# One load per float64 weight piece in 1 KB packets, the power of two in two ScalarE passes, and the sums of pair 4 off TensorE

## The chip, the cores and the metric

The kernel runs on one core of one Trainium2 chip. The metric is the device time of one execution in microseconds (us). The engines, by the names that the profile uses: PE is TensorE (matmuls; PEld is its weight load), DVE is VectorE, ACT is ScalarE, POOL is GpSimd and SP is SyncE, which here only issues DMAs. A name with a q (SPq, POOLq) is an engine's queue of DMA issues. Every engine works through its own instructions strictly in the order in which they were written; engines wait for each other by semaphores.

## The reference

Two blocks in a row. The first is attention with a threshold: for 8 batches of 8 heads, 576 positions and 64 values a head,

```
scores = scale * q @ k.T
thresh = max(scores, axis=-1) - tau
scores = where(scores >= thresh, scores, -1e9)
attn   = exp(scores - max(scores));  attn /= sum(attn) + 1e-9
x      = attn @ v                     # then (B,H,S,D) -> (4608, 512)
```

The second is a feed-forward block on the 4608 rows of x:

```
h = x @ w_in                          # 512 -> 2048
g = h * 1 / (1 + exp(-1.702 * h))
out = g @ w_out                       # 2048 -> 512
```

q, k and v are float32. The two weight matrices reach the kernel as float64, and the kernel turns them into float32 itself, from their bits.

## The kernel before

**Attention.** Work goes by pairs of heads: four pairs a batch, 32 in all. The first four pairs (batch 0) go a straight way, in 20 units (pair n, tile t of 128 queries): scores on PE (L668), row maxima (L678) and a bias (L683) on DVE, the mask (L689) and the exponentials with their sums (L697) on ACT, a transposition on PE (L708, L709), copies of it on ACT (L718, L726), a small reciprocal on DVE (L732, L733), its spread over partitions by matmuls with the identity (`straight_den`, L745) and the values (`straight_values`, L758) on PE. `straight_spread` (L764, ACT) copies the spread reciprocals into the block's input xT and `straight_place` (L768, DVE) multiplies the values into it. Both matmul groups of a unit write the same PSUM tile, `small`, of which there are two buffers, shared with the feed-forward block.

From pair 4 on the scores stay transposed. PE makes them (L540), ACT copies them out (`keep`, L557), DVE takes maxima by groups of 32 (L563) and folds them, and for nearly all pairs the row of maxima goes to DRAM (L613) and comes back broadcast over 64 partitions (`row_in`, L622; the profile writes arena<-row). DVE subtracts it (`sub`, L627), ACT masks (L633) and exponentiates (L637), PE multiplies with the values (L779). The sums of the exponentials take one of two ways. Pairs from 5 on: DVE adds by groups (L563 again), `turn_sums` (L828 to L833) makes the reciprocals, `sums_out` (L838) writes them to DRAM and `sums_in` (L845) reads them back broadcast, both on SP. Pair 4 alone: `sums_by_pe`, 36 matmuls with a matrix of ones (tile den, L779), then `one_row` (L802, L806) and `spread_sums` (L854, L856) on DVE. `place_x` (L871) multiplies values by reciprocals into xT. From pair 7 on PE's values of pair n-2 alternate with the scores of pair n.

**Feed-forward.** 18 blocks of 256 rows. Blocks 0 and 1 are plain: `mm1_0` (L929) for 16 chunks of 128 hidden values, tanh on ACT (L895), gelu on DVE (L935), then `mm2` (L908). Chunks 4c to 4c+3 of the hidden values need four pieces of w_in; the second layer needs w_out by rows. Block 2 and later blocks (L886, gelu L898, L1080) use Strassen-like products whose weight sums are made by ACT (L1036) and by accumulating DMAs from POOL (L1040, 1 MB each). Block 2 holds rows of batch 1, so it needs pairs 4 to 7 placed.

**Weights.** There are 32 pieces of 128 x 512 float64 values, 16 of w_in and 16 of w_out. A piece is loaded twice from POOL's queue (`load_w`, L466 and L467): once as words and once shifted by three bytes, so that the top 28 bits of the fraction line up in a word. The pieces lie in six places until they are converted: four in rows of w_out that are not yet filled ("stage"), two in the arena ("w64"). DVE takes the exponent (`cv_ex`, L477), ACT makes the power of two from it with one Relu (`cv_power`, L485, on every other word), DVE cuts and signs the fraction (`cv_frac`, L491 and L495) and multiplies (`cv_end`, L503). The first six loads wait until k of pair 3 has been prepared (`hold`).

**Order.** Nothing is ordered by hand. `run_in_order` is a planner: it plays the tasks through with given costs, takes on each engine the ready task of lowest rank, and writes the instructions in that order. Ranks are a base for each pair or piece (S_RANK, W_RANK) plus an offset for each kind of task (EARLY, SECOND, LATER, CV). The tasks of the feed-forward block on PE have the last rank (LAST) and so fill what attention leaves. Transfers are modelled by two movers, SP's (DMS) and the weights' (DMW), that share bandwidth by SHARE.

Of the kernel before, what the change touches and what calls it, by code (L numbers as in the profile page):

```python
# [10 lines left out]
FP32 = mybir.dt.float32  # L11
# [8 lines left out]
P = 128  # L20
# [10 lines left out]
def kernel(  # L31
# [98 lines left out]
    for x in ("P0", "P1", "P2", "PT0", "PT1"):  # L130
# [3 lines left out]
        "load_qk": 3.49,  # L134
        "load_v": 61.83,
        "prep": 15.43,
        "straight_bias": -0.96,
        "straight_copy": -11.35,
        "straight_copy1": 16.32,
        "straight_den": 8.82,  # L140
        "straight_exps": 28.06,
        "straight_mask": -43.64,
        "straight_max": 14.96,
        "straight_place": -2.45,
        "straight_rc": 26.0,
        "straight_scores": -15.67,
        "straight_spread": 28.02,
        "straight_turn": 5.62,
        "straight_values": 34.4,
        "w_sum": 16.49,  # L150
    }
    SECOND = {
        "exps": 53.1,
        "in_groups": 125.36,
        "keep": 24.5,
        "load_qk": 15.38,
        "load_v": 40.57,
        "mask": 51.96,
        "one_row": 31.95,
        "over_halves": -45.57,  # L160
        "over_tiles": 26.99,
        "place_x": 1.35,
        "prep": 9.24,
        "row_in": 57.1,
        "row_out": -10.1,
        "scores_run": -13.37,
        "spread_sums": 38.44,
        "sub": 49.29,
        "sums_by_pe": 66.1,
        "sums_in": 49.6,  # L170
        "sums_out": -47.62,
        "turn_rows": -10.91,
        "turn_sums": 11.87,
        "values": 17.4,
    }
    LATER = {
        "exps": 41.63,
        "in_groups": 59.97,
        "keep": 8.55,
        "load_qk": 30.71,  # L180
        "load_v": 52.56,
        "mask": 61.02,
        "over_halves": -20.34,
        "over_tiles": 9.26,
        "place_x": -2.55,
        "prep": -8.58,
        "row_in": -50.04,
        "row_out": -53.37,
        "scores_run": 26.7,
        "sub": 15.31,  # L190
        "sums_in": 13.02,
        "sums_out": 33.45,
        "turn_rows": 7.35,
        "turn_sums": 21.37,
        "values": 50.74,
        "x_sum": 55.75,
    }
# [10 lines left out]
    MODES = {"scores_run": 1, "values": 1, "sums_by_pe": 1, "straight_scores": 1, "straight_values": 2, "straight_den": 2}  # L208
# [15 lines left out]
    SHARE = (0.055, 0.3)  # L224
# [98 lines left out]
    rebias = const.tile([P, 1], FP32, name="rebias")  # L323
    JOINT = 7
# [101 lines left out]
    cv, turn = {}, {"w64": 0}  # L426
# [3 lines left out]
    PER_STAGE = NFC // STAGES  # L430

    def stage(i):
# [6 lines left out]
    for x in range(STAGES):  # L439
        limits[f"stage{x}"] = 1  # L440

    def load_w(i):
        dst, src, c, j = pieces[i]
        dram = src[ts(c, P), ts(j, WC)]
        if not wide:
            nc.gpsimd.dma_start(out=dst[:, c, ts(j, WC)], in_=dram)
            return


        x = stage(i)  # L450
        if x is None:
            o = 4 * WC * (turn["w64"] % 2)
            turn["w64"] += 1
            t, t3 = (
                arena[:, ds(o + 2 * WC * y, 2 * WC)].bitcast(U32).rearrange(
                    "p (c w) -> p c w", w=2
                )
                for y in range(2)
            )
        else:  # L460
            rows = [w_out[:, ds(PER_STAGE * x + 2 * y, 2), :] for y in range(2)]
            t, t3 = (
                r.rearrange("p a b -> p (a b)").bitcast(U32).rearrange("p (c w) -> p c w", w=2)
                for r in rows
            )
        nc.gpsimd.dma_start(out=t.rearrange("p c w -> p (c w)"), in_=dram.bitcast(U32))  # L466
        nc.gpsimd.dma_start(  # L467
            out=t3.rearrange("p c w -> p (c w)").bitcast(U8)[:, 0 : 8 * WC - 3],
            in_=dram.bitcast(U8)[:, 3 : 8 * WC],
        )  # L470
        cv[i] = t[:, :, 1], t[:, :, 0], t3[:, :, 0]
# [3 lines left out]
    def cv_ex(i):  # L475
        hi, ex, _ = cv[i]
        nc.vector.tensor_scalar(  # L477
            out=ex, in0=hi, scalar1=20, scalar2=0x7FF,
            op0=ALU.logical_shift_right, op1=ALU.bitwise_and,
        )  # L480

    def cv_power(i):

        ex = cv[i][1].bitcast(I32)
        nc.scalar.activation(out=ex, in_=ex, func=AF.Relu, scale=2.0**23, bias=rebias)  # L485

    def cv_frac(i):


        hi, _, frac = cv[i]  # L490
        nc.vector.tensor_scalar(  # L491
            out=frac.bitcast(I32), in0=frac.bitcast(I32), scalar1=0x0FFFFFFF,
# [659 lines left out]

    SUMS_BY_PE = (4,)
    BY_DMA = (0, 1, *range(3, NP))
    SUMS_BY_DMA = range(5, NP)
    LEAD = 6
# [457 lines left out]
```

## Time and profile before

| | |
|---|---|
| median of 3 runs | 1329.69 us (1327.19 to 1330.22) |
| the profiled execution | 1330.04 us, span 1328.3 us |
| mean granted TensorE clock | 0.988 |
| PE busy | 1282.8 us (97%) |
| DVE, ACT, POOL busy | 981.8 us (74%), 662.1 us (50%), 250.3 us (19%) |
| DMA | 102.91 MB; POOL's software queue 37.74 MB, SP's queue 63.40 MB |

Times in the profile are us from the first instruction. A row of a group of instructions reads: line, engine, operation, out<-in with shapes, count | busy us, mean ns of one | idle time of that engine just before them, and what ended it. A busy PE is not a PE at its peak, since matmuls overlap and their ends are modelled. Idle time of an engine that does not set the end costs nothing.

### The profile page before, as it was taken

How to read it: one execution, taken by the hardware profiler on the slowest of the kernel's cores; microseconds unless marked ns; L12 is line 12 of the kernel's file. 1: busy time of each engine (PE TensorE's matmuls, PEld its weight loads, DVE VectorE, ACT ScalarE, POOL GpSimd, SP SyncE). 2: the span in 40 equal slices, each digit the busy share in tenths (PEclk: the TensorE clock that was granted, in tenths of full speed). 3: DMA queues.
4: the chain of work that ended last, by engine and by line, in shares of the span. 5: the costliest groups of instructions: out<-in, count | busy, mean ns of one | idle time of the engine just before them, and what ended most of it. 6: DMA issues, size and time to landing. Idle time of an engine off the chain costs nothing.

```text
span 1328.3 us, 23115 instructions
## 1 busy us (share of the span) xinstructions
PE 1282.8 (97%) x9212; PEld 999.9 (75%) x9212; DVE 981.8 (74%) x1640; ACT 662.1 (50%) x922; POOL 250.3 (19%) x296
## 2 busy tenths in 40 slices
PE   6798989897999999999999999999999999999998
PEld 3576664456777777777888777777777878888887
DVE  6888887987788888777787777778887873652642
ACT  6897665676455555555455545455555540210210
POOL 2111210002113120212120202112111217120120
PEclk9899999898999999999999999999999999999999
DMA  8786767256221222222222222212222110000000
GB/s 173 211 303 172 259 185 126 62 108 107 59 67 49 68 48 66 48 54 53 71 55 71 55 70 55 65 42 57 59 46 57 33 53 9 17 0 25 9 0 32
DMA packets 194949, 102.91 MB, mean 77 GB/s; under 512 B 160282, under 2 KB 173338, under 8 KB 194842
## 3 DMA queue, kind: packets, MB, share of 16 engines
q1 hardware_dynamic: 181114, 63.40, 20.4%
q0 software_dynamic: 11360, 37.74, 9.5%
q8 instruction: 72, 1.18, 0.4%
q10 hardware_dynamic: 2368, 0.30, 0.2%
q14 instruction: 35, 0.29, 0.1%
HBM read 87.51 MB, written 9.69 MB: 73 GB/s over the span
## 4 chain that ended last, share of the span: by engine, by line
PE 78%; DVE 7%; DMA 7%; SPq 4%; ACT 3%; issue 1%; DVEq 0%; ACTq 0%
PE ops L1080 24%; PE hps L886 22%; PE pv L779 8%; PE ps L540 8%; PE ps L994 4%; PE ps L1080 4%; PE ops L994 3%; PE hps L929 3%; SPq L393 2%; DMA arena<-row 2%; DVE arena L627 2%; DVE part L563 2%; DMA arena<-in_k_dram 2%; DMA row<-flat 1%; PE rest L758 1%
## 5 line engine op out<-in xcount | busy, mean ns | idle before, releaser
L563 DVE TRANSPOSE_TENSOR_REDUCE part<-arena 128x36 f32<-128x1152 f32 x275 | 334.5, 1238 | 46.3 <-ACT arena L557 36.9
L886 PE MATMUL hps<-xT,w_in 128*128 128x256 f32 x1536 | 339.7, 382 | 6.9 <-DVE arena L898 6.9
L886 PEld LDWEIGHTS hps<-xT,w_in 128*128 128x128 f32 x1536 | 292.3, 191 | 53.2 <-DVE arena L898 7.9
L633 ACT ACTIVATE arena<-arena 128x1152 f32<-128x1152 f32 (+1 forms) x140 | 147.6, 1059 | 155.6 <-DVE arena L627 155.5
L1080 PE MATMUL ops<-w_out,arena 128*128 128x256 f32 x896 | 202.7, 381 | 1.0 <-DVE arena L898 0.9
L627 DVE TENSOR_TENSOR arena<-arena 128x1152 f32<-128x1152 f32 (+1 forms) x140 | 178.1, 1313 | 26.7 <-DMA arena<-row 26.6
L557 ACT COPY arena<-ps 128x576 f32<-128x576 f32 x252 | 149.9, 642 | 94.6 <-PE ps L540 92.8
L1080 PEld LDWEIGHTS ops<-w_out,arena 128*128 128x128 f32 x896 | 169.1, 190 | 28.7 <-DVE arena L898 3.1
L637 ACT ACTIVATE arena<-arena,shift,scl 128x1152 f32<-128x1152 f32 (+1 forms) x140 | 174.5, 1250 | 3.0
L1046 POOL TENSOR_TENSOR arena<-arena 128x256 f32<-128x256 f32 x56 | 50.3, 897 | 644.7 <-DVE arena L898 542.9
L540 PE MATMUL ps<-arena 64*64 64x288 f32 x2016 | 150.5, 411 | 5.2 <-ACT arena L557 5.2
L895 ACT ACTIVATE th<-hps 128x512 f32<-128x512 f32 x112 | 66.3, 592 | 170.9 <-PE hps L886 156.6
L1080 PE MATMUL ops<-arena 128*128 128x256 f32 x672 | 150.6, 380 | 0.0
L779 PE MATMUL pv<-arena 64*64 64x288 f32 x2016 | 147.7, 407 | 0.0
L1080 PEld LDWEIGHTS ops<-arena 128*128 128x128 f32 x672 | 127.2, 190 | 19.3 <-issue 2.2
L540 PEld LDWEIGHTS ps<-arena 64*64 64x64 f32 x2016 | 74.2, 135 | 57.1 <-ACT arena L557 15.9
L1102 DVE SCALAR_TENSOR_TENSOR osb<-ops,osb 128x256 f32<-128x256 f32 x98 | 39.3, 413 | 100.0 <-PE ops L1080 93.8
L779 PEld LDWEIGHTS pv<-arena 64*64 64x64 f32 x2016 | 74.7, 134 | 50.9 <-issue 10.0
L898 DVE SCALAR_TENSOR_TENSOR arena<-th,hps 128x512 f32<-128x512 f32 x96 | 64.4, 671 | 38.6 <-ACT th L895 38.4
L929 PE MATMUL hps<-xT,w_in 128*128 128x256 f32 x256 | 62.9, 400 | 7.7 <-DVE arena L935 7.4
L929 PEld LDWEIGHTS hps<-xT,w_in 128*128 128x128 f32 x256 | 49.4, 199 | 19.3 <-DVE arena L935 8.9
L524 DVE STREAM_TRANSPOSE arena<-arena 128x576 f32<-128x576 f32 x60 | 42.9, 746 | 22.1 <-DMA arena<-in_k_dram 11.1
(134 smaller groups left out, 1267.2 us busy)
## 6 DMA issues: line engine op xcount, KB each, us to landing
arena<-in_v_dram SPq DMA_DIRECT2D x112, 144.0 KB
arena<-in_q_dram SPq DMA_DIRECT2D x128, 72.0 KB
out_dram<-osb SPq DMA_DIRECT2D x36, 256.0 KB
arena<-in_k_dram SPq DMA_DIRECT2D x124, 72.0 KB
arena<-row SPq DMA_DIRECT2D x56, 144.0 KB
arena<-row_s SPq DMA_DIRECT2D x54, 144.0 KB
w_out<-in_moe_w_in_dram POOLq DMA_DIRECT2D x12, 512.0 KB, 8.9
arena<-in_moe_w_out_dram POOLq DMA_DIRECT2D x12, 512.0 KB, 5.8
```

What stands on the lines that cost most here:

```text
L540: nc.tensor.matmul(ps[ts(c, KT), h, 0:SH], lhsT=mats[n, 1][ts(h, D), ts(j, KT)], rhs=mats[n, 0][ts(h, D), ts(c, SH)], start=True, stop=True,)
L557: nc.scalar.copy(out=sT[n, t][:, u], in_=pss.pop((n, j))[:, :, 0:SH])
L563: nc.vector.tensor_reduce(out=stats[n, op][:, t * 2 * QB : min(2 * t + 2, NK) * QB], in_=sT[n, t].rearrange("p u h (g d) -> p (u h g) d", ...
L627: nc.vector.tensor_tensor(out=s, in0=s, in1=mbs[n].unsqueeze(1).to_broadcast(list(s.shape)), op=ALU.subtract)
L633: nc.scalar.activation(out=s, in_=s, func=AF.Prelu, alpha=STEEP)
L637: nc.scalar.activation(out=s, in_=s, func=AF.Exp, scale=scl, bias=shift)
L779: nc.tensor.matmul(o[c][ts(h, D), 0:SH], lhsT=left(j, h)[ts(c, KT)], rhs=sT[n, t][ts(c, KT), u, h, :], start=(j == 0), stop=(j == NK - 1),)
L886: nc.tensor.matmul(hidden[j][:, ts(f, BLK)], lhsT=w_in[:, c, ds((f * HF + j) * P, P)], rhs=xTs[blk][:, c, :], start=(c == 0), stop=(c == N ...
L895: nc.scalar.activation(out=ths[j], in_=hidden[j], func=AF.Tanh, scale=GELU_SCALE / 2)
L929: nc.tensor.matmul(hidden[j // 2][:, ts(j % 2, BLK)], lhsT=w_in[:, c, ts(j, P)], rhs=xTs[i][:, c, :], start=(c == 0), stop=(c == NDC - 1),)
L994: nc.tensor.matmul(places[j, x], lhsT=left[:, c, ts(j, P)], rhs=right[:, c, :], start=(c == 0), stop=(c == 1),)
L1080: nc.tensor.matmul(banks[blk][k][:, ts(o, HM)], lhsT=left[:, j, :], rhs=right[:, j, :], start=(j == 0), stop=(j == HF - 1),)
```

## The change

A piece is loaded once, cut into packets of 1 KB instead of the 4 KB of a partition's row. Without the shifted copy each stage holds two pieces, and the arena four: twelve places. The conversion changes. DVE shifts the high word right with its sign (`cv_ex`, straight into the destination); ACT makes the signed power of two from it in two Prelu passes, in place, the second with integer output; DVE puts the leading one on the fraction's high part (`cv_frac`), joins the low word (`cv_join`) and multiplies (`cv_end`). That is still four DVE instructions for a piece, and two ACT instructions instead of one. A w_out piece's first conversion step now waits until its destination rows are free of staged pieces.

`straight_den` goes as a task; its matmuls are issued at the end of `straight_values`, and `straight_spread` follows that. Pair 4's sums take the way of the later pairs (`SUMS_BY_PE` is empty, `SUMS_BY_DMA` begins at 4). The planner gets other ranks for all kinds of tasks, other costs for several, and other shares of bandwidth. The diff, cut to its core:

```diff
     EARLY = {
-        "load_qk": 3.49,
-        "load_v": 61.83,
...
+        "load_qk": -6.99,
+        "load_v": 19.38,
...
     CV = {
-        "cv_end": 43.69,
-        "cv_ex": 42.76,
-        "cv_frac": 5.16,
-        "cv_power": 29.72,
-        "load_w": 7.92,
+        "cv_end": -7.74,
+        "cv_ex": -36.17,
+        "cv_frac": 2.14,
+        "cv_join": -50.97,
+        "cv_power": 117.41,
+        "cv_power2": 87.54,
+        "load_w": 4.35,
     }
...
-    SHARE = (0.055, 0.3)
+    SHARE = (0.22, 0.6)
...
+    HALVES = [f"stage{x}{y}" for x in range(STAGES) for y in range(2)]
+    W64 = [f"w64_{x}" for x in range(4)]
...
+    def staged(i):
         if i < n_in:
-            return i % (STAGES + 2) if i % (STAGES + 2) < STAGES else None
+            every = HALVES[:4] + W64[:2] + HALVES[4:] + W64[2:]
+            return every[i % len(every)]
         i -= n_in
-        return STAGES - 1 if i % 3 == 0 and i < NFC - PER_STAGE else None
+        return HALVES[6 + i // 3 % 2] if i % 3 == 0 and i < NFC - PER_STAGE else W64[(i - i // 3) % 4]
...
-        nc.gpsimd.dma_start(out=t.rearrange("p c w -> p (c w)"), in_=dram.bitcast(U32))
-        nc.gpsimd.dma_start(
-            out=t3.rearrange("p c w -> p (c w)").bitcast(U8)[:, 0 : 8 * WC - 3],
-            in_=dram.bitcast(U8)[:, 3 : 8 * WC],
-        )
-        cv[i] = t[:, :, 1], t[:, :, 0], t3[:, :, 0]
+        nc.gpsimd.dma_start(out=t, in_=dram.bitcast(U32), max_dma_last_dim=1024)
+        t = t.rearrange("p (c w) -> p c w", w=2)
+        cv[i] = t[:, :, 1], t[:, :, 0], dst[:, c, ts(j, WC)]

     def cv_ex(i):
+        hi, _, o = cv[i]
+        nc.vector.tensor_single_scalar(
+            out=o.bitcast(I32), in_=hi.bitcast(I32), scalar=20, op=ALU.arith_shift_right
+        )
+
+    def cv_power(i):
+        o = cv[i][2]
+        nc.scalar.activation(out=o, in_=o.bitcast(I32), func=AF.Prelu, bias=rebias, alpha=2.0**-40)
+
+    def cv_power2(i):
+        o = cv[i][2]
+        nc.scalar.activation(
+            out=o.bitcast(I32), in_=o, func=AF.Prelu, bias=rebias2, scale=2.0**23, alpha=2.0**40
+        )
+
+    def cv_frac(i):
+        hi = cv[i][0]
         nc.vector.tensor_scalar(
-            out=ex, in0=hi, scalar1=20, scalar2=0x7FF,
-            op0=ALU.logical_shift_right, op1=ALU.bitwise_and,
-        )
...
+            out=hi.bitcast(I32), in0=hi.bitcast(I32), scalar1=0x000FFFFF, scalar2=0x00100000,
+            op0=ALU.bitwise_and, op1=ALU.bitwise_or,
+        )
+
+    def cv_join(i):
+        hi, lo, _ = cv[i]
         nc.vector.scalar_tensor_tensor(
-            out=frac.bitcast(I32), in0=hi.bitcast(I32), scalar=31, in1=frac.bitcast(I32),
-            op0=ALU.arith_shift_right, op1=ALU.bitwise_xor,
+            out=hi.bitcast(FP32), in0=lo, scalar=2.0**-32, in1=hi.bitcast(I32),
+            op0=ALU.mult, op1=ALU.add,
         )
...
-    def straight_den(n, t):
...
     def straight_values(n, t):
...
+        for h in range(2):
+            r = figures(n, t, 3)[:, h % heads(t) : h % heads(t) + 1]
+            nc.tensor.matmul(
+                small[n, t][ts(h, D), ds(3 * P, k)], lhsT=r.to_broadcast([P, D]),
+                rhs=eye if heads(t) == 2 else eye[:, ts(h, k)], start=True, stop=True,
+            )
...
-    nc.gpsimd.memset(rebias, -896.0 * 2.0**23)
+    nc.gpsimd.memset(rebias, -896.0)
+    nc.gpsimd.memset(rebias2, 1792.0 * 2.0**-17)
...
-    SUMS_BY_PE = (4,)
+    SUMS_BY_PE = ()
     BY_DMA = (0, 1, *range(3, NP))
-    SUMS_BY_DMA = range(5, NP)
+    SUMS_BY_DMA = range(4, NP)
...
-    W_RANK = (12.68, 4.74, -9.33, 15.31, 8.01, 7.11)
+    W_RANK = (-53.35, -5.67, 56.61, 61.89, -5.56, 48.51)
+    W_TIME = 1.9
...
-        a = transfer("DMW", 3.4, a)
-        e = task("DVE", 0.34, rank, cv_ex, i, after=[a])
+        a = transfer("DMW", W_TIME, a)
+
+        over = [
+            ready_w[y] for y in range(i)
+            if i >= n_in and staged(y) in HALVES[2 * ((i - n_in) // PER_STAGE) :][:2]
+        ]
+        e = task("DVE", 0.33, rank, cv_ex, i, after=[a] + over)
         m = task("ACT", 0.67, rank, cv_power, i, after=[e])
-        a = task("DVE", 1.05, rank, cv_frac, i, after=[e])
...
+        m = task("ACT", 0.67, rank, cv_power2, i, after=[m])
+        a = task("DVE", 0.42, rank, cv_frac, i, after=[e])
+        a = task("DVE", 0.61, rank, cv_join, i, after=[a])
+        ready_w.append(task("DVE", 0.61, rank, cv_end, i, after=[a, m], give=place))
...
-    S_RANK = (-1.44, 2.78, 7.37)
+    S_RANK = (-4.42, -17.19, 4.68)
```

More of the change, by code (lines that the diff above doesn't have):

```diff
@@ L151 @@
+        "w_sum": 90.41,
     }
     SECOND = {
[L153 to L174, printed above, removed]
+        "exps": -8.01,
+        "in_groups": 121.89,
+        "keep": 8.52,
+        "load_qk": -60.94,
+        "load_v": 127.47,
+        "mask": 92.02,
+        "over_halves": -26.23,
+        "over_tiles": -53.86,
+        "place_x": -40.91,
+        "prep": 109.09,
+        "row_in": -38.28,
+        "row_out": 19.96,
+        "scores_run": -1.49,
+        "sub": 24.27,
@@ L175 @@
+        "sums_in": 27.21,
+        "sums_out": -40.63,
+        "turn_rows": -31.38,
+        "turn_sums": 97.65,
+        "values": 117.99,
     }
     LATER = {
[L177 to L196, printed above, removed]
+        "exps": 26.76,
+        "in_groups": 140.58,
+        "keep": -31.05,
+        "load_qk": 105.64,
+        "load_v": 65.31,
+        "mask": 18.17,
+        "over_halves": -22.78,
+        "over_tiles": 5.19,
+        "place_x": -61.68,
+        "prep": -28.15,
+        "row_in": -9.02,
+        "row_out": 27.42,
@@ L739, in at @@
         return xTs[blk][:, n, ds(off, P // (3 - heads(t)))]
-    def straight_den(n, t):
-        k = P // (3 - heads(t))
-        for h in range(2):
-            r = figures(n, t, 3)[:, h % heads(t) : h % heads(t) + 1]
-            nc.tensor.matmul(
-                small[n, t][ts(h, D), ds(3 * P, k)], lhsT=r.to_broadcast([P, D]),
-                rhs=eye if heads(t) == 2 else eye[:, ts(h, k)], start=True, stop=True,
-            )
     def straight_values(n, t):
```

112 lines of the change are left out of this document (48 added, 64 removed).

## The prediction

> **What bounds the kernel now.** The page's totals come first, then the same busy times by stage, because a share of 97% says nothing of where the other 3% lies.
>
> ```profile
> span 1328.3 us, 23115 instructions
> PE 1282.8 (97%) x9212; PEld 999.9 (75%) x9212; DVE 981.8 (74%) x1640; ACT 662.1 (50%) x922; POOL 250.3 (19%) x296
> ```
> ```profile
> 20.00:60.00 40.00, 30.49 (x345) 20.02 (x347) 30.73 (x79) 35.57 (x69) 7.99 (x15) 0.87 0.80 221
> 60.00:120.00 60.00, 58.47 (x637) 43.09 (x633) 52.72 (x122) 53.30 (x105) 14.51 (x27) 1.00 0.73 248
> 120.00:200.00 80.00, 71.48 (x571) 53.80 (x573) 67.38 (x125) 51.31 (x75) 13.40 (x24) 0.96 0.72 216
> 200.00:260.00 60.00, 54.79 (x334) 26.02 (x327) 49.91 (x71) 37.48 (x45) 3.18 (x2) 0.94 0.52 99
> 260.00:340.00 80.00, 73.12 (x522) 48.69 (x524) 65.36 (x102) 52.65 (x63) 14.29 (x14) 0.96 0.48 93
> 340.00:1300.00 960.00, 959.01 (x6644) 781.06 (x6637) 699.26 (x1106) 422.07 (x551) 192.43 (x198) 1.00 0.19 47
> ```
> Each row of the second block is a stretch of the span: its length, the busy time of PE, PE's weight loads, DVE, ACT and POOL, then the granted TensorE clock, the share of the DMA engines and GB/s. From 340 to 1300 us PE is busy 959 of 960 us, so nothing done to another engine there can pay. PE's idle time is 1328.3 - 1282.8 = 45.5 us, and nearly all of it lies before 340 us, where all of the change but its new order works. So the time is taken as PE's busy time plus its idle time: work taken off PE counts in full, and elsewhere only an idle gap that closes or opens counts.
>
> The third view is PE's waits before 340 us (waiting line, what released it, total, times, longest):
>
> ```profile
> PE ps L668 <- DVE arena L518: 8.5, 1, 8.5
> PE hps L929 <- DVE arena L935: 7.4, 3, 3.6
> PE hps L886 <- DVE arena L898: 6.9, 2, 6.0
> PE rest L758 <- DMA arena<-in_v_dram: 5.8, 3, 4.1
> PE ps L540 <- ACT arena L557: 5.2, 1, 5.2
> ...
> PE rest L758 <- ACT xT L764: 1.1, 1, 1.1
> ```
> The 8.5 us is the start, before any weight is loaded, and stays. The chain of waits, in order of time, says what stands behind the others:
>
> ```profile
> 112.21 9.40 DMA arena<-row
> ...
> 158.71 12.01 DMA arena<-row
> ...
> 234.54 3.28 DMA arena<-row
> ```
> The spread of a row of maxima (row) takes 9.40 and 12.01 us while weights are being loaded, and 3.28 us at 234 us, when they are in. At 121.7 and 170.8 us the DVE goes on with a subtraction that waited for it; the gelu (L935) for which PE waits stands behind that subtraction in the DVE's queue. So most of the 7.4 us is a DMA wait in disguise, and the 5.8 us at L758 is one openly.
>
> **The change part by part.** The sum is made against the profiled execution, 1330.04 us (0.35 above the median, 1329.69). A measurement here can tell some 0.2% from no change, 2.7 us.
>
> *Pair 4's sums leave PE.* Its 36 matmuls on ones, in 72 records, go:
>
> ```profile
> L779 PE MATMUL den<-arena,ones 64*64 64x288 f32 x72 | 4.5, 402 | 0.0
> ...
> L563 DVE TRANSPOSE_TENSOR_REDUCE part<-arena 128x36 f32<-128x1152 f32 (+1 forms) x61 | 72.9, 1232 | 4.6 <-ACT arena L557 4.6
> ...
> L802 DVE TRANSPOSE_TENSOR_REDUCE r<-den 128x9 f32<-128x288 f32 x2 | 0.8, 462 | 2.1 <-PE den L779 2.1
> ```
> **-4.5 us**, in full. In exchange the DVE gets five reductions by L563, four of 1152 and one of 576 as in that group, about 5 x 1.23 = 6.2 us, and loses 0.8 us and a wait of 2.1 us. Net 5.4 us more, beside 12.6 us that the DVE idles in 120 to 200; it is hidden there, and exposed if the gaps behind the late row close: ends 0 and +5.4, taken 0, since the DVE's idle time is the larger. The SP queue gets four more issues and one more in-order wait, with the q and k loads of later pairs behind it:
>
> ```profile
> SPq L838 <- DVE flat_s L833: 44.9, 5, 23.8
> ```
> Five such waits held the queue 9.0 us on average (44.9/5). No PE wait above names a load behind them: 0 taken, +9.0 as the other end.
>
> *Weights are loaded once.* 32 pieces of 512 KB instead of 64. The first burst keeps its size: twelve buffers of 0.5 MB now, six pieces of 1 MB before, after the same gate (pair 3's prepared k). But 1 KB packets stand beside the attention's small ones, not 4 KB packets, and the later traffic halves. The rows at 112 and 158 us should come down from 9.40 and 12.01 towards 3.28: 6.1 and 8.7 us less, more than the 3.6 us (the longest) and a middle one, (7.4 - 3.6)/2 = 1.9, for which PE waited. **-5.5 us**; ends 0 (packets do not help) and -7.4. The V wait, 5.8 us, goes too, but the gain is not PE's: in 20 to 60 ACT is busy 35.57 of 40, so at most 4.4 us can be pulled forward, and the second pass takes most of it (below). **-1.0 us**; ends +2 and -5.8. Issuing costs POOL nothing that counts: two issues of 0.57 us become one, with four times the packets in it; even at four times the time that is 2.3 us for 1.1, on an engine busy 19%.
>
> ```profile
> L466 POOL DMA_DIRECT2D w_out<-in_moe_w_in_dram x12 | 6.8, 567 | 36.5 <-DVE w_in L503 23.9 <-ACT arena L718 7.8 <-DVE xT L768 4.6
> ```
> *Power in two passes.* The DVE keeps four instructions of the same sizes for a piece (one shift, one mask, two with two operands): 0. ACT gets one pass more. The old pass reads every other word; the new ones read closed rows:
>
> ```profile
> 20.00:120.00 100.00, 12.94 (x17) 0.95 0.76 237
> ```
> ```profile
> L485 ACT ACTIVATE arena<-arena,rebias 128x512 int32<-128x512 int32 x16 | 12.5, 794 | 4.4 <-DVE arena L477 4.4
> ...
> L895 ACT ACTIVATE th<-hps 128x512 f32<-128x512 f32 x24 | 14.3, 595 | 18.1 <-PE hps L929 13.7 <-PE hps L886 4.1
> ...
> L689 ACT ACTIVATE arena<-ps,stat 128x576 f32<-128x576 f32 x36 | 26.1, 736 | 13.4 <-DVE stat L683 12.7 <-PE ps L708 0.7
> ```
> The window row counts L485 alone: 17 of the 32 pieces pass ACT between 20 and 120 us. A new pass lies between 0.595 (L895, as long) and 0.794 us (L485). L689 is the nearest, the same Prelu with a bias by partition, 576 long: 0.736 x 512/576 = 0.65 as the low reading, 0.736 as the high; I take 0.68. A piece then costs 2 x 0.68 - 0.79 = 0.57 us more, all of them 18 us (12.7 to 25.4 by the ends), and the 17 of the early stretch 9.7 us. ACT idles 4.4 + 6.7 = 11.1 us in that stretch, so the cover just holds, and six pieces before 60 us (3.4 us) eat the 4.4 that the V wait would give back: hence the 1.0. Taken 0 beyond this; ends 0 and +18. The cover is better than it looks, because PE has used only 64 records of the first layer by then:
>
> ```profile
> 20.00:120.00 100.00, 15.65 (x64) 11.51 (x64) 0.95 0.76 237
> ```
> This row counts L929 alone: 64 records are 8 of the 16 hidden chunks of the first block, so 8 pieces were needed and 17 were converted.
>
> The Trainium skill, page "ScalarE: Activation LUTs", section "What ACT_TABLE_LOAD costs", gives 280 ns + 0.833 ns an element with a bias operand by partition: an estimate of 0.707 us for a pass of 512 and 20 us over 32 pieces in place of my 18. The L689 row agrees with it within 0.03 us (the page gives 0.760 for 576), and with it the early stretch would need 10.6 of the 11.1 us.
>
> *Sums spread with the values.* The matmuls of the reciprocals move into the values' task, and their copy (L764) comes after it. PE's 1.1 us at L758 behind that copy goes; each of 20 units now ends one copy later.
>
> ```profile
> L764 ACT COPY xT<-rest 128x128 f32<-128x128 f32 (+1 forms) x20 | 5.1, 274 | 1.7 <-PE rest L758 1.6
> ```
> **-1.1 us**; the other end is 20 x 0.27 = +5.4, if the two buffers behind it run out.
>
> *Clock.* Stretches with idle gaps run PE below full clock:
>
> ```profile
> 120.00:140.00 20.00, 16.37 (x116) 12.62 (x116) 16.37 (x30) 15.02 (x23) 3.18 (x6) 0.91 0.77 205
> ```
> It holds the 3.6 us wait; without it 9% of 16.4 us, **-1.5 us**, come back.
>
> *New ranks* reorder every queue and cannot be costed by instruction. Ends: the two later waits (6.9 + 5.2 = 12.1 us), behind gelu and copies, all gone, or as much again opened. Taken 0, as the reason of neither is in the change.
>
> Sum: 1330.0 - 4.5 - 5.5 - 1.0 - 1.1 - 1.5 = 1316.4 us, 1.0% below before.
>
> **The rivals.** *More gain.* If the new order also takes the later waits, 12.1 us, the time is 1304; half of it, 1310. For it: shorter rows let the pairs run ahead. The clock adds: 13% of 30.5 us and 6% of 54.8, some 7 us, if all gaps close. The Trainium skill, page "TensorE: Matmul & The Clock Gate", section "Part 1: The HAM clock gate", halves the clock after an idle window of about 3.4 us; the 0.87 of 20 to 60, and 1.00 of 60 to 120 where PE idles 1.5 us in all, agree. Against it: both waits come after the weights are in. 0.22.
>
> *Pair 7 binds.* Block 2 needs pair 7 placed:
>
> ```profile
> 278.30 0.51 DVE xT L871 x2
> ```
> ```profile
> 287.48 1.89 PE L886 MATMUL hps<-xT,w_in 128*128 128x256 f32 x8
> ```
> Block 2 starts 8.7 us after it. Should pair 7 not come earlier, PE's filler ends first and the gain stops at 8.7: 1321. Against it: its chain passes the same slow rows. 0.16.
>
> *The loads are not lighter.* The copy of 1 MB in rows shows a slow case:
>
> ```profile
> arena<-w_out POOLq DMA_DIRECT2D x3, 1024.0 KB, 9.8
> ```
> At that rate a piece takes 4.9 us, against 4.2 for its 1 MB at 248 GB/s. Rows and V stay late: 1330.0 - 4.5 - 1.1 = 1324. Against it: that copy also accumulates. 0.08.
>
> *ScalarE becomes the bound (the other side).* It is at 89% from 20 to 120. If its added 18 us stand ahead of the masks and exponentials there, every unit of the first batch, and with it pairs 4 to 7, moves by that: 1316.4 + 18 = 1334, at the upper price 1342. It decides from 13.6 - 2.7 = 11 us exposed for "no gain" and 16.3 for a loss. For it: the cover of 11.1 us is nearly used up. Against it: 15 pieces fall after 120, where ACT idles 28.7 of 80 us. Slower 0.19; partly exposed, within 0.2%, 0.09.
>
> **How the numbers follow.** The forecast has 0.26 and its own range is 1312 to 1320. Faster: 0.26 + 0.22 + 0.16 + 0.08 = 0.72; same 0.09; slower 0.19. The range runs from all later waits and a third of the clock's 7 us gone (1302) to ScalarE fully exposed at the middle price (1334): it leaves out some 0.05 below and 0.11 above.
>
> **What would show it.** Right: no den matmuls; row spreads before 200 us near 3 to 5 us; PE idle from 20 to 340 us about 24 us instead of the 31.7 of the five rows; no wait of L758 for V above 2 us. Wrong: ACT above 95% from 20 to 120 with PE waiting for masks or exponentials; a new wait for converted weights at the first layer; the row spread still at 9 us; a gap after block 1 before block 2.

## The result, and the profile after

The changed kernel takes 1315.70 us (median of four runs, 1315.47 to 1317.27) against 1328.44 us for the kernel before beside it (four runs, 1326.42 to 1330.22). The ratio is 0.9907, with a 95% interval of 0.9888 to 0.9926: 12.7 us or 0.9% less, where 1316.4 us had been forecast. The total was met almost exactly (the gain less well, 12.7 us for 13.6), the terms of the sum were not: two misses of opposite sign nearly cancel in the trace, so the closeness is in part luck.

The page of the changed kernel has these totals; the second fence is its table by stretches, with the same columns as before (length, busy time of PE, PE's weight loads, DVE, ACT and POOL, granted clock, DMA share, GB/s):

```profile
span 1315.5 us, 22946 instructions
PE 1275.2 (97%) x9140; PEld 994.8 (76%) x9140; DVE 987.2 (75%) x1648; ACT 675.9 (51%) x954; POOL 241.8 (18%) x265
```
```profile
20.00:60.00 40.00, 26.23 (x258) 19.61 (x258) 25.16 (x66) 27.02 (x53) 11.35 (x16) 0.79 0.84 243
60.00:120.00 60.00, 57.10 (x605) 41.00 (x604) 49.77 (x118) 59.02 (x117) 5.23 (x7) 1.00 0.33 92
120.00:200.00 80.00, 75.73 (x585) 54.08 (x581) 75.88 (x139) 67.72 (x108) 7.50 (x10) 1.00 0.42 112
200.00:260.00 60.00, 55.09 (x337) 26.27 (x339) 52.90 (x75) 40.81 (x48) 3.17 (x2) 0.97 0.52 103
260.00:340.00 80.00, 80.00 (x680) 55.77 (x673) 73.48 (x121) 51.32 (x68) 15.83 (x15) 1.00 0.52 104
```
The span fell by 12.8 us: PE's busy time by 7.6 (1282.8 to 1275.2, in which the 4.5 us of the den matmuls are), and its idle time by 5.2 (45.5 to 40.3). The five rows say where the idle time went, as length minus PE's busy time, before and after:

| stretch, us | idle before | idle after | difference |
|---|---|---|---|
| 20 to 60 | 9.5 | 13.8 | +4.3 |
| 60 to 120 | 1.5 | 2.9 | +1.4 |
| 120 to 200 | 8.5 | 4.3 | -4.2 |
| 200 to 260 | 5.2 | 4.9 | -0.3 |
| 260 to 340 | 6.9 | 0.0 | -6.9 |

The first stretch got worse: PE does 4.3 us less there, at a granted clock of 0.79 in place of 0.87. The gain was made after 120 us. PE's waits before 340 us give the gaps names (waiting line, what released it, total, times, longest):

```profile
PE rest L740 <- DMA arena<-in_v_dram: 10.3, 1, 10.3
PE ps L659 <- DVE arena L509: 8.0, 1, 8.0
PE ps L531 <- ACT arena L548: 4.9, 1, 4.9
...
PE hps L917 <- DVE arena L923: 2.4, 4, 0.9
...
PE ops L896 <- DVE arena L923: 1.1, 1, 1.1
```
The lines have moved: L740 is the values' matmul (L758 before), L917 the first layer of the first block (L929), L923 its gelu (L935), L896 the second layer (L908), L531 the scores (L540), L874 the first layer of the other blocks (L886), L618 the subtraction that waits for the row (L627). The start (8.0) and the scores' wait (4.9, 5.2 before) are as they were. The gelu's wait fell from 7.4 to 2.4, or 3.5 with the 1.1 of the second layer. The later wait of 6.9 us (L886) and the 1.1 us behind the spread copy (L764) are gone. But the wait for V, which should have fallen, is 10.3 us in one piece instead of 5.8 in three. A timeline of SP's queue, which issues the small loads in order, shows what V stands behind (start, length, line, transfer):

```profile
13.98 2.26 SPq L392 DMA_DIRECT2D arena<-in_q_dram  x4
...
19.00 5.12 SPq L406 DMA_DIRECT2D arena<-in_v_dram  x8
24.25 11.10 SPq L392 DMA_DIRECT2D arena<-in_q_dram  x4
35.45 14.80 SPq L392 DMA_DIRECT2D arena<-in_k_dram  x4
50.34 22.55 SPq L406 DMA_DIRECT2D arena<-in_v_dram  x16
```
V of pairs 0 and 1 is issued at 19.0 us, q and k of pair 4 at 24.3 and 35.5, and V of pairs 2 and 3 only from 50.3 (the first 8 of the last row's 16). Four issues of a q take 2.26 us at 14 us and 11.10 at 24 us, once the weights' burst has begun (21.6 us). Pair 4 was loaded first, while PE stood still for pair 2's V from 45.4 to 55.7 us. The last rows that the argument needs are the two passes of the power, here two of ACT's four groups of them:

```profile
L470 ACT ACTIVATE w_in<-w_in,rebias 128x512 f32<-128x512 int32 x16 | 11.7, 733 | 0.0
L474 ACT ACTIVATE w_out<-w_out,rebias 128x512 int32<-128x512 f32 x16 | 11.7, 732 | 0.3
```

### The profile page after: what moved, and what is told of

It is laid out like the page before. It is cut to its first block, busy times and chain, and to the rows that moved or that the text cites. A ratio compares the mean times of both kernels' runs of the same rounds, so it can differ in the third digit from the quotient of the medians.

```text
span 1315.5 us, 22946 instructions
## 1 busy us (share of the span) xinstructions
PE 1275.2 (97%) x9140; PEld 994.8 (76%) x9140; DVE 987.2 (75%) x1648; ACT 675.9 (51%) x954; POOL 241.8 (18%) x265
## 4 chain that ended last, share of the span: by engine, by line
PE 79%; DVE 6%; ACT 5%; DMA 4%; issue 3%; SPq 1%; POOL 0%; DVEq 0%; POOLq 0%; ACTq 0%
PE ops L1068 25%; PE hps L874 24%; PE pv L767 9%; PE ps L531 8%; PE ps L982 4%; PE ps L1068 4%; PE ops L982 3%; PE ops L896 2%; DVE arena L618 2%; ACT arena L628 1%; SPq L392 1%; DMA arena<-in_moe_w_in_dram 1%; ACT arena L624 1%; ACT arena L548 1%; DVE part L554 1%
## 5 line engine op out<-in xcount | busy, mean ns | idle before, releaser
L554 DVE TRANSPOSE_TENSOR_REDUCE part<-arena 128x36 f32<-128x1152 f32 (+1 forms) x280 | 338.2, 1234 | 43.8 <-ACT arena L548 24.0
L874 PE MATMUL hps<-xT,w_in 128*128 128x256 f32 x1536 | 336.7, 380 | 0.0
L874 PEld LDWEIGHTS hps<-xT,w_in 128*128 128x128 f32 x1536 | 290.8, 190 | 44.7 <-issue 5.7
L624 ACT ACTIVATE arena<-arena 128x1152 f32<-128x1152 f32 (+1 forms) x140 | 144.3, 1061 | 140.8 <-DVE arena L618 139.9
L618 DVE TENSOR_TENSOR arena<-arena 128x1152 f32<-128x1152 f32 (+1 forms) x140 | 179.8, 1326 | 14.8 <-DMA arena<-row 14.8
L628 ACT ACTIVATE arena<-arena,shift,scl 128x1152 f32<-128x1152 f32 (+1 forms) x140 | 170.0, 1246 | 1.2
L531 PE MATMUL ps<-arena 64*64 64x288 f32 x2016 | 151.0, 408 | 6.3 <-ACT arena L548 4.9
L531 PEld LDWEIGHTS ps<-arena 64*64 64x64 f32 x2016 | 72.7, 133 | 58.1 <-ACT arena L548 16.8
L886 DVE SCALAR_TENSOR_TENSOR arena<-th,hps 128x512 f32<-128x512 f32 x96 | 64.5, 672 | 45.5 <-ACT th L883 45.3
L917 PE MATMUL hps<-xT,w_in 128*128 128x256 f32 x256 | 60.8, 387 | 3.4 <-DVE arena L923 2.4
L917 PEld LDWEIGHTS hps<-xT,w_in 128*128 128x128 f32 x256 | 46.8, 190 | 16.2 <-DVE arena L923 5.8
L1047 POOL TENSOR_TENSOR arena<-arena 128x512 f32<-128x512 f32 x28 | 38.1, 1363 | 113.1 <-PE ops L1068 113.1
```

Source lines behind the costliest of these rows:

```text
L531: nc.tensor.matmul(ps[ts(c, KT), h, 0:SH], lhsT=mats[n, 1][ts(h, D), ts(j, KT)], rhs=mats[n, 0][ts(h, D), ts(c, SH)], start=True, stop=True,)
L554: nc.vector.tensor_reduce(out=stats[n, op][:, t * 2 * QB : min(2 * t + 2, NK) * QB], in_=sT[n, t].rearrange("p u h (g d) -> p (u h g) d", ...
L618: nc.vector.tensor_tensor(out=s, in0=s, in1=mbs[n].unsqueeze(1).to_broadcast(list(s.shape)), op=ALU.subtract)
L624: nc.scalar.activation(out=s, in_=s, func=AF.Prelu, alpha=STEEP)
L628: nc.scalar.activation(out=s, in_=s, func=AF.Exp, scale=scl, bias=shift)
L874: nc.tensor.matmul(hidden[j][:, ts(f, BLK)], lhsT=w_in[:, c, ds((f * HF + j) * P, P)], rhs=xTs[blk][:, c, :], start=(c == 0), stop=(c == N ...
```

## The experiments

Each kernel was run beside the kernel before on the same chip, and its time is given as the difference to that one's median (1327.39 to 1328.23 us, by chip); on this scale, against its own 1328.44, the change itself stands at -12.7 us. Three theories run through them, named by words because every expectation letters its own: **the queue**, the order in SP's queue under the burst makes the V wait; **the next wait**, another takes its place when it goes; **the fit**, the ranks fit only the code that they were found for. Beside them stands what each part of the change is worth by itself.

**1. The loads not cut (a_4kb).** The changed kernel with each load in its natural form.

```diff
-nc.gpsimd.dma_start(out=t, in_=dram.bitcast(U32), max_dma_last_dim=1024)
+nc.gpsimd.dma_start(out=t, in_=dram.bitcast(U32))
```


> The changed kernel with its weight loads not cut: a partition's row of 4 KB is one piece instead of four of 1 KB; nothing else differs, and every engine's order is the same. Theory A (halving the bytes is what counts, the cutting does nothing): 1315.7 us within 2.7, the SP queue still needs about 11 to 15 us for the four issues of pair 4's q and of its k during the first burst, and the wait for V stays near 10 us. Theory B (the smaller packets give the small transfers their share): those issues and the V wait grow by half or more, the row spreads before 200 us go back towards 9 us, and the time rises by 3 to 6 us.

1313.87 us, ratio 0.9895 (0.9877 to 0.9913), -14.4 us: not to be told from the change itself (0.9888 to 0.9926). DMA packets between 15 and 60 us, first of the changed kernel, then of this one (queue, packets, MB, share of 16 engines):

```profile
q0 software_dynamic: 2160, 7.87, 54.0%
```
```profile
q0 software_dynamic: 2160, 7.87, 49.4%
```
The same 2160 packets carry the same bytes, 3.6 KB each, cut or not. What the cut shows in is the issues. POOL's (L455) takes 0.75 us with it in the changed kernel and 0.53 here, and in this profile SP's four issues of pair 4's k are shorter and PE's wait for V is less than half:

```profile
34.56 11.29 SPq L392 DMA_DIRECT2D arena<-in_k_dram  x4
```
```profile
PE rest L740 <- DMA arena<-in_v_dram: 4.6, 1, 4.6
```
The time is where theory A of the expectation has it, but the wait neither stayed near 10 us, as A had it, nor grew, as B had it. The profiles of the kernels with cut loads, the change and numbers 4 and 12, have 14.80 to 14.89 us for that k and 9.7 to 10.5 us of V wait, so if the cut does anything to SP's queue, it holds it up. But this profile is of the fastest of four runs (1309.86 us; the others 1313.52 to 1314.27), and a gain in time is not shown. So "1 KB packets stand beside the attention's small ones" is not what the profile shows. The Trainium skill, page "DMA: Bandwidth & Descriptors", section "SWDGE vs HWDGE vs iDMA", makes the packet the point at which a DMA engine changes its queue, of preferably up to 4096 bytes and 64 descriptors; with 3.6 KB a packet the trace agrees with the size; no run here shows the change of queue.

**2. V ahead of pair 4, first try (a_v_first).** V of pairs 2 and 3 is issued before q and k of pair 4. In this form pair 2's V also comes ahead, in the program, of the matmuls that read pair 0's V in the same buffer, so those matmuls read pair 2's values.

```diff
 def load_qk(n, which, queue):
+    if n == NPAIR and which == 0:
+        load_v(2), load_v(3)
```


> The changed kernel with the V loads of pairs 2 and 3 issued on SP's queue ahead of q and k of pair 4, instead of behind them; the orders of all other engines are the same. In the changed kernel TensorE waits 10.3 us for this V, and ScalarE and VectorE stand still with it from 48 to 58 us. Theory A (the wait is the in-order SP queue: V stands behind eight slow issues): the wait falls under 3 us and 7 to 10 us of the time go with it, 1306 to 1309 us. Theory B (V is late because the weights' burst holds the DMA engines, wherever V stands): the wait stays at 5 us or more and the time within 1312 to 1317. Theory C (ScalarE, 98% busy from 60 to 120 us, takes the gain back): the wait goes, and the time still falls by less than 3 us.

1316.53 us, ratio 0.9915 (0.9899 to 0.993), -11.7 us, and `PE rest L740` still waits 10.8 us for V. The experiment moved the wait to an earlier matmul (PE stands from 23.4 us on, before the values of pair 0) instead of removing it, and decides nothing. Number 5 does it without this fault.

**3. Every piece moved twice (a_two_loads).** Each piece is also copied from its place in DRAM to a spare one there; that is the bytes of the old second load, but not its destination.

```diff
+nc.gpsimd.dma_start(
+    out=spares.tile([P, 2 * WC], U32, name=f"spare{i}", ...),
+    in_=dram.bitcast(U32), max_dma_last_dim=1024)
```


> The changed kernel with the bytes of the double load put back: behind each weight load, a copy of the same piece goes to a spare place in DRAM, which nothing reads. All engines but POOL keep their order. Theory A (half the bytes shortened the rows and with them the gelu waits): row spreads before 200 us go back to about 9 us, the waits of TensorE for gelu from 3.5 to 7 us or more, and the time rises by 4 to 8 us, to 1320 to 1324. Theory B (the new order closed those gaps): the time stays within 2.7 us of 1315.7.

1339.14 us, ratio 1.009 (1.0072 to 1.0109), +10.9 us, so 23.6 us more than the change. PE's waits before 340 us, and SP's queue, of this kernel:

```profile
PE rest L740 <- DMA arena<-in_v_dram: 28.0, 1, 28.0
...
PE hps L917 <- DVE arena L923: 6.5, 5, 2.5
```
```profile
35.22 25.48 SPq L392 DMA_DIRECT2D arena<-in_k_dram  x4
60.80 21.28 SPq L406 DMA_DIRECT2D arena<-in_v_dram  x12
```
With more weight traffic in flight the same four k issues take 25.48 us instead of 14.80, V is issued 10.5 us later, and its wait grows by 17.7 us. The queue theory gains. What had been expected was smaller and of another kind: the gelu's waits did rise, from 3.5 to 7.8 us with the 1.3 of the second layer, but the DVE waits only 3.0 us for rows here, 4.7 in the change.

**4. One pass of ACT left out (a_one_pass).** `cv_power2` returns at once.

```diff
 def cv_power2(i):
+    return
```


> The changed kernel without the second ScalarE pass: the power of two stays unfinished, so the converted weights are wrong in scale. It leaves out 32 x 0.73 = 23 us of ScalarE's work, 12 of the passes (8.6 us) between 60 and 120 us, where ScalarE is 98% busy. Theory A (the pass is covered there, as the prediction has it): 1313 to 1316 us. Theory B (ScalarE bounds that stretch and its passes move pairs 4 to 7): 6 us or more faster, 1310 or less.

1312.75 us, ratio 0.9884 (0.9868 to 0.9899), -15.5 us: 2.8 us better than the change, with intervals that overlap, for 32 x 0.73 = 23 us less ACT work. The row of this kernel from 60 to 120 us and its longest wait:

```profile
60.00:120.00 60.00, 57.81 (x614) 41.75 (x611) 50.79 (x121) 52.96 (x108) 5.22 (x7) 1.00 0.33 93
```
```profile
PE rest L740 <- DMA arena<-in_v_dram: 10.5, 1, 10.5
```
ACT is busy 52.96 of 60 us instead of 59.02 and PE gains 0.7 us there. The V wait stays at 10.5: the second pass had no part in it.

**5. q and k of pair 4 after V (a_qk_later).** As number 2 meant it: the loads of pair 4 are put off until V of pair 3 has been issued. The other engines keep their order.

```diff
 def load_qk(n, which, queue):
+    if n == NPAIR and late[0]:
+        return late.append((n, which, queue))
...
 def load_v(n):
     ...
+    return n == 3 and after_v3()      # issues what was put off
```


> The changed kernel with q and k of pair 4 issued on SP's queue after the V of pairs 2 and 3 instead of before; this V still comes behind the matmuls that read the buffer's last user, and all other engines keep their order. Theory A (V waits behind eight slow issues in SP's in-order queue): TensorE's wait for V falls from 10.3 us to under 3, the still time of ScalarE and VectorE from 48 to 58 us goes, and the time falls by 6 to 10 us, to 1306 to 1310. Theory B (V is late because the burst of weights holds the DMA engines): the wait stays above 5 us, and the time is 1313 to 1317. Theory C (ScalarE takes the gain back between 60 and 120 us): the wait goes and less than 3 us of the time with it.

**1304.10 us** (1301.51 to 1305.02), ratio 0.9824 (0.98 to 0.9848), -23.3 us: 10.6 us better than the change, and better than both kernels. SP's queue, the first stretch and the wait of this kernel:

```profile
18.85 18.91 SPq L406 DMA_DIRECT2D arena<-in_v_dram  x16
37.86 9.34 SPq L392 DMA_DIRECT2D arena<-in_q_dram  x4
47.30 5.90 SPq L392 DMA_DIRECT2D arena<-in_k_dram  x4
```
```profile
20.00:60.00 40.00, 32.84 (x384) 23.33 (x384) 35.51 (x95) 38.53 (x76) 12.31 (x17) 1.00 0.89 252
```
```profile
PE rest L740 <- DMA arena<-in_v_dram: 1.3, 1, 1.3
```
All V of pairs 0 to 3 is issued by 37.8 us, the wait falls from 10.3 to 1.3 us, PE works 6.6 us more in 20 to 60, and its clock there is 1.00 instead of 0.79. The weights' burst is the same (2160 packets, 7.87 MB between 15 and 60 us). The two profiled executions lie farther apart than the medians, 15.8 us of span: 9.0 are this wait, and 5.4 are busy time of the same 9140 matmuls, at a mean clock of 1.000 for 0.992. The queue theory holds for the changed kernel, and no next wait takes the place there.

**6. Both (a_both).** Numbers 1 and 5 in one.

> The same, and the weight loads not cut into 1 KB. If the cutting only costs (POOL's issue 0.75 us against 0.53, and the V wait 10.3 against 4.6 us in the profile without it) the two add up where they have not the same wait to win: 1 to 3 us under the run with q and k later alone, 1304 to 1309 us. If both win by the one V wait, this is within 1.5 us of that run.

1303.73 us, ratio 0.9821 (0.9801 to 0.9842), -23.7 us, the same as number 5. With V early, cutting the loads or not makes no difference.

**7 and 8. The ranks exchanged (a_old_ranks, b_new_ranks).** The changed code with the ranks of before, and the code before with the new ranks. Only ranks are exchanged; each code keeps its planner's costs and shares of bandwidth.

> The changed code with the ranks of the kernel before (all tables, W_RANK, S_RANK); the two new tasks of the conversion get the ranks of the steps that they follow. Theory A (the code pays, by bytes and by pair 4's sums; the order is worth little): 1314 to 1321 us, without the den matmuls and with TensorE's waits for gelu before 200 us under 4 us. Theory B (the new order closed the gaps after 120 us, above all the 6.9 us at block 2): 1323 us or more, with waits of TensorE for gelu between 120 and 340 us back at 8 us or more.

> The kernel before with the ranks of the changed one; tasks that only it has keep their ranks. Theory A (the order is worth little by itself): 1326 to 1331 us. Theory B (the order closed the gaps): 1318 to 1324. Theory C (the ranks only fit the code that they were made for): slower than 1332.

1352.96 us, ratio 1.0188 (1.0168 to 1.0209), +25.6 us; and 1338.62 us, ratio 1.0086 (1.0063 to 1.0108), +11.2 us. From 20 to 340 us, the longest waits of the first, and the longest of the second:

```profile
PE ps L663 <- ACT arena L684: 15.3, 7, 11.4
PE rest L704 <- DVE xT L760: 13.8, 4, 10.5
PE rest L744 <- ACT arena L721: 9.8, 3, 7.6
```
```profile
PE ps L537 <- DVE arena L521: 24.9, 1, 24.9
```
Each set of ranks opens waits of 10 to 25 us in the other code. The new ranks are worth 38 us on the new code and cost 11 on the old: the fit holds, and "new ranks 0" was no fair way to write that term. The 38 is against ranks that partly had to be borrowed, since two tasks of the new conversion have none in the old set. And SP's queue has a part in the two longest waits, as the chains of the two runs show, first of number 7 and then of number 8:

```profile
27.95 18.96 DMA arena<-in_q_dram
```
```profile
39.68 13.80 SPq L390
```
In number 7 the DVE stands 11.7 us for that q of pair 4, with the maxima behind it that PE's 11.4 us are waiting for. In number 8 a single issue of pair 4's k takes 13.80 us; there the DVE converts weights from 60.7 to 75.3 us while PE waits, so queue and order are not separated. Part of what the ranks are worth is thus the place of these loads.

**9. One load, in the old kernel (b_one_load).** The kernel before with its second, shifted load of each piece dropped and the place of it set to zero once; same orders.

```diff
-nc.gpsimd.dma_start(...)        # the shifted U8 load of each piece
+[nc.gpsimd.memset(z, 0.0) for z in [...]]     # once, at the start
```


> The kernel before without the second, shifted load of each piece; its place is set to zero once at the start, so the fractions of the weights are not those of the reference. Nothing else differs, and SP, ScalarE, TensorE and VectorE keep the order of the kernel before. It measures half the bytes alone. Theory A (the prediction's: the row spreads of 9.4 and 12.0 us shrink towards 3.3, the gelu waits of 7.4 us fall under 3, the V wait of 5.8 falls too): 1318 to 1323 us. Theory B (the order, not the bytes, made the gaps): the waits stay within 2 us of 7.4 and 5.8, and the time within 2.7 us of the kernel before.

1316.50 us, ratio 0.9917 (0.9902 to 0.9931), -11.5 us. Its waits, and the rows on its chain:

```profile
PE hps L886 <- DVE arena L898: 7.5, 2, 6.0
...
PE hps L929 <- DVE arena L935: 2.5, 2, 1.6
```
```profile
108.26 7.36 DMA arena<-row
...
151.38 8.72 DMA arena<-row
```
Half the bytes take the V wait away altogether and the gelu's from 7.4 to 2.5 us, but the spreads of a row are still at 7.36 and 8.72 us (9.40 and 12.01 with two loads), and the later wait stays at 7.5. SP's queue, first of the kernel before and then of this one, shows how the V wait goes:

```profile
24.55 14.29 SPq L393 DMA_DIRECT2D arena<-in_q_dram  x4
38.94 8.00 SPq L393 DMA_DIRECT2D arena<-in_k_dram  x4
47.04 5.07 SPq L407 DMA_DIRECT2D arena<-in_v_dram  x8
```
```profile
24.93 7.66 SPq L393 DMA_DIRECT2D arena<-in_q_dram  x4
32.69 5.38 SPq L393 DMA_DIRECT2D arena<-in_k_dram  x4
38.16 5.07 SPq L407 DMA_DIRECT2D arena<-in_v_dram  x8
```
The order is the same, but the issues of q and k are shorter, so V of pairs 2 and 3 is issued 8.9 us earlier. PE's busy time falls by 6.0 us (1282.8 to 1276.8) with the same 9212 matmuls, at a mean clock of 0.995 for 0.988; that is half of the gain.

**10. q and k later, in the old kernel (b_qk_later).** The edit of number 5 in the kernel before.

> The kernel before with q and k of pair 4 issued on SP's queue after the V of pairs 2 and 3; all other engines keep their order. In the kernel before TensorE has the scores of pair 4 from 53.7 us on, in the changed one from 89 us on. Theory A (the V wait is the queue here too, and costs what it shows): the 5.8 us of V wait fall under 2, and the time to 1320 to 1324. Theory B (here the scores of pair 4 need what was put back): a new wait of TensorE for pair 4's q or k of 3 us or more takes the place of the V wait, and the time is 1326 to 1336.

1327.84 us, ratio 1.0003 (0.9993 to 1.0013): nothing. V's wait falls to 1.0 us, and this takes its place:

```profile
PE ps L540 <- DVE stat L732: 4.7, 1, 4.7
```
Here the next wait holds: the DVE comes to that step (L732) only after it has waited 1.4 us for a q and 2.1 us for a k, so with two loads and the old order PE's next work is not ready either.

**11 and 12. Pair 4's sums by themselves (b_sums_dma, a_sums_pe).** The kernel before with these sums moved to the DVE and a DMA, and the changed kernel with them back on PE.

```diff
-SUMS_BY_PE, SUMS_BY_DMA = (4,), range(5, NP)
+SUMS_BY_PE, SUMS_BY_DMA = (), range(4, NP)       # number 11; number 12 the reverse
```


> The kernel before with pair 4's sums made by VectorE and spread by DMA, as the changed kernel does it; the planner reorders what follows. Theory A (work off TensorE counts in full): 4.5 us less, 1322 to 1326 us, with TensorE's busy time 4 to 5 us lower. Theory B (the added work on VectorE and SP's queue opens a gap as long): busy time lower by 4 to 5 us and idle time higher by 3 or more, 1326 us or above.

> The changed kernel with pair 4's sums on TensorE again, as in the kernel before, and the rest of the planner's order following. Theory A (4.5 us in full): 1319 to 1322 us. Theory B (the gain is lost or doubled in the order around it): under 1317 or above 1325.

1316.93 us, ratio 0.9919 (0.9904 to 0.9933), -11.1 us; and 1323.53 us, ratio 0.9969 (0.9958 to 0.998), -4.5 us, so 8.2 us worse than the change. In both the planner reorders the other tasks as well. The two totals, and the waits of number 11:

```profile
PE 1277.2 (97%) x9140; PEld 993.4 (76%) x9140; DVE 984.8 (75%) x1648; ACT 659.6 (50%) x922; POOL 249.4 (19%) x296
```
```profile
PE 1282.1 (97%) x9212; PEld 997.9 (76%) x9212; DVE 985.0 (75%) x1640; ACT 672.8 (51%) x954; POOL 240.1 (18%) x265
```
```profile
PE hps L886 <- DVE arena L898: 3.9, 2, 3.5
...
PE hps L929 <- DVE arena L935: 2.7, 1, 2.7
```
PE's busy time moves by 5.6 and 6.9 us, about the 4.5 and the clock's share. The rest is waiting: in number 11 the gelu's goes from 7.4 to 2.7 and the later one from 6.9 to 3.9. The DVE's busy time rises by 3.0 us in number 11 and falls by 2.2 in number 12.

## Why the prediction was right, and where it was not

The forecast (1316.4, faster) held, and the mechanism, PE's busy time less the den matmuls plus fewer gaps before 340 us, is what the trace shows: PE idles 25.9 us there, for 31.7 before and 24 forecast. Of the signs named for it, one failed: V's wait is 10.3 us and not under 2. The row spreads before 200 us are not decided by the changed kernel's chain, on which none stands there (one of 7.40 us stands at 223.65 us). Of the signs named against it none came up: ACT is at 98% from 60 to 120 us but at 86% over the 20 to 120 us that were named, and there PE waits 4.3 us for masks, against 4.1 for masks and exponentials before; no wait for converted weights is seen, and the gap before block 2 is closed.

Of the rivals, ScalarE as the bound is answered by number 4. Pair 7 does not bind: it is placed by 275.8 us and block 2 starts at 283.8, with PE never idle from 260 to 340. "More gain" came true in part, since the wait before L886 went and the one before the scores stayed (5.2 to 4.9); that number 5 reaches its 1304 us is chance, because it does so by the V wait. By its steps:

| step | forecast | in the trace of the change | tried alone |
|---|---|---|---|
| den matmuls | -4.5 | x72 gone | -11.1 (in before), 8.2 if undone |
| DVE's reductions | +5.4 busy, 0 | +5.4 busy, conversion included | +3.0 and 2.2 busy (numbers 11, 12) |
| rows and gelu | -5.5 | gelu 7.4 to 3.5 | -11.5 with V (in before) |
| V | -1.0 | 5.8 to 10.3: +4.5 | 10.6 to be had (in after) |
| second pass | 0 | 0.73 us a pass | 2.8, not clear of noise |
| spread with values | -1.1 | -1.1 | not tried |
| clock | -1.5 | -3.1, by subtraction | not tried |
| new ranks | 0 | later wait 6.9 to 0 | +38 and +11 exchanged |

*The den matmuls were mis-sized.* The 4.5 us are PE's own, and the step left out that the waits after the sums change too. With the planner's reordering the move alone is worth 11.1 us; in its profile PE's busy time falls by 5.6 us and the gelu's and the later wait by 4.7 + 3.0. Whether the sums themselves stood in the way or the reordering did it is not separated. The added DVE work was hidden as forecast, but it is 2 to 3 us and not 5.4: the forecast took off only the reduction on den and not the other steps of the old way, and that the whole change has 5.4 is in part chance.

*Rows and gelu:* right in kind, smaller than forecast in this order (3.9 us by the waits), and its reason only half right. The spreads did not come near 3.28 us (7.36 and 8.72 in number 9). What the DVE waits for them in 20 to 345 us, before and after, is the better measure (5.1 in number 9):

```profile
DVE arena L627 <- DMA arena<-row: 12.3, 4, 4.9
```
```profile
DVE arena L618 <- DMA arena<-row: 4.7, 3, 3.2
```

*V is the step that failed.* It was put at -1.0, between +2 and -5.8, because ACT was thought to cap it; it came out at +4.5, beyond the upper end, and number 4 shows that the second pass had no part. The forecast took the V wait for a matter of bytes. With half the bytes and the old order it does vanish, because SP's issues get shorter (number 9); in the new order it hangs on SP's queue, where the loads for scores that PE reaches at 89 us stand ahead of one that it needs at 45 (number 5), with longer issues the more weight traffic there is (number 3). Nor did the first burst keep its size: between 15 and 60 us 7.87 MB of weights moved, 6.29 before, since three more loads begin as places come free. The q and k of pair 4 stood ahead before, too (issued at 24.55 and 38.94 us); there the old order had scores of that pair for PE from 53.7 us on, and the new order has them at 89 us.

*The second pass* was rightly taken at nothing. A pass took 0.73 us instead of 0.68; the four groups come to 46.7 us where one pass took 24.8, so 21.9 us more and not 18, and all but 2.8 us of the second pass at most are covered. The Trainium skill, page "ScalarE: Activation LUTs", section "What ACT_TABLE_LOAD costs", gave an estimate of 0.707 us from its figures; the rows above are 4% over it and 8% over the forecast's value.

*The clock* gave 3.1 us net, if all that PE's busy time lost beyond the 4.5 is put down to it. The 120 to 200 stretch went from 0.96 to 1.00 as forecast, and 20 to 60 lost.

*New ranks:* the term was bounded by 12.1 us on both sides, and the runs give 38 and 11. What went with the new order was the later wait of 6.9 us: it stays in number 9 (7.5), half of it stays in number 11 (3.9), and it is 0.6 in number 12, which has the new order with the sums back on PE. But the new code with the old ranks has only 2.4 of it (number 7), so the order is not all of it. Which of the moved tasks did it is not isolated.

Two misses nearly cancel, and that is luck: V came out 5.5 us worse than forecast (+4.5 for -1.0), and the later wait 6.9 us better. The parts alone come to -11.5 - 11.1 = -22.6 us, the change gave -12.7, and with V's place in the queue mended -23.3. This fits a change whose parts nearly add and which gave 10.6 us back to one wait that its own new order made longer; the sum is no proof, since the order differs between these runs.

Left open: merging the reciprocal sums into the values' task was not tried by itself, and that SP's issues slow under a burst was seen, not explained.

## What to carry to other kernels

When a bulk load runs beside an in-order queue of small loads, list what stands in that queue behind the burst's start and when each is first read: an exchange in that order was worth 10.6 us here, where the whole change was worth 12.7, and nothing in the kernel before, where another wait stood behind (number 10). Cost a moved operation by the waits that end behind it as well as by its own time. Ranks of a written-out order belong to their code; take them over into another version only with a new search, and don't read a part's worth from a version whose order was made for another.

## What the runs showed of the hardware that was not expected

The issue of a small DMA on SP is not of fixed length. Four q issues took 2.26 us before the weights' burst and 11.10 with it in flight, four k issues 2.67, 14.80, and 25.48 with each piece copied besides; that last is 6.4 us an issue, and a single one took 13.80 us in number 8. Cutting a load's rows to 1 KB left packets and bytes as they were (2160 packets, 7.87 MB in 45 us) and made its issue on POOL longer, 0.75 us for 0.53. In the 10 us in which PE waits for V the other engines stand as well, as the row of 48 to 58 us of the changed kernel shows, and then that of number 5 (PE, PE's loads, DVE, ACT, POOL):

```profile
48.00:58.00 10.00, 2.26 (x20) 2.19 (x22) 0.60 (x1) 0.00 (x0) 0.75 (x1) 0.60 0.63 147
```
```profile
48.00:58.00 10.00, 8.70 (x98) 6.04 (x98) 9.76 (x25) 9.82 (x21) 0.75 (x1) 1.00 0.79 156
```
The first runs at a granted clock of 0.60, the second at 1.00: one late load left three engines nearly idle, and cost PE its clock besides.
